# Second group's keys, grams and inversion ahead of the first FFN block of a delta rule with two FFN layers

## The chip, the cores and the metric

One core of one Trainium2 chip runs the whole program. Five engines work side by side, each through its own queue in order: TensorE (PE, matrix products; PEld is its weight load), VectorE (DVE), ScalarE (ACT), GpSimd (POOL) and SyncE (SP, which here only issues DMAs). An engine waits for another by semaphores. The metric is the time of one execution on the device in microseconds; lower is better.

## What is computed

```python
k_n = k / (norm(k) + 1e-6)                    # (4, 8, 768, 48): batch, head, time, dim
for t in range(768):                          # the delta rule, one state (48 x 48) per batch and head
    y[t]  = q[t] @ state
    v_old = state.T @ k_n[t]
    state = state + beta[t] * outer(k_n[t], v[t] - v_old)
x = y as (3072 tokens, 384)
h = x @ w_in                                  # (384, 2048)
g = 0 below -1, (h + 1)**2 / 4 between, h above 1
x = g @ w_out                                 # (2048, 384)
h = x @ w_in2;  g = relu(h)**2;  out = g @ w_out2
```

The time loop is done in 24 chunks of 32 steps. Within a chunk the steps depend on each other through a triangular matrix per batch and head, which is inverted; between chunks they depend through the state.

## The kernel before

**Chunks and groups.** A chunk holds 32 time steps of all 32 batch-head pairs. Chunks are gathered in groups of 2, 4, 4, 4, 4, 4, 2 (`GROUPS`). For each chunk `gram(c)` makes the products of keys with keys and of queries with keys on PE (L302, 64 matmuls), ACT or DVE takes them out of PSUM, and a mask is multiplied in (L318, on POOL where `eng=G`). For each group `tri(n, eng)` inverts all its triangles at once: `begin` transposes the grams to `gm` (L394, DVE), `pre` makes norms and scales two matrices (L266 to L434), `steps` is a chain of `tensor_mul` to `t` and `tensor_add` to `tx` (L454, L455), and `end` transposes back (L458). Groups 0 and 1 are done in halves (28 instructions instead of 60), with two small products for the rest: `rows` transposes `d` (L483), `ld` makes `z` (L487), `dld` makes `w` (L495) and subtracts it (L500). Group 0 is inverted on DVE, all later groups on POOL.

**A chunk's chain.** `chunk_steps(c)` gives six steps, called ks, tr, qs, ku, pu, xt below: what the state already predicts is subtracted from the value (L532), the inverse is applied (L536, copied by ACT L544), the output is made (L522, L556, copied by L560), the state moves on (L567, copied by L572 and L573), and `xt` turns the output into the FFN's input, a high part `xh` and a low part `xl` in fp32r (L590 to L593). Its tr needs the inverse of the chunk's group; `value(c)` (L278, POOL) multiplies the norms into the values.

**FFN units.** The FFN runs in blocks of chunks (`SIZES` 2, 2, 3, ...) and, in a block, in 16 units, one for each 128 columns of the hidden width. `unit(x)` does `hidden` (nine matmuls to `h`, then r on ACT L631, g on DVE L632, ACT L634, DVE L635), `rest` (high part `gh` on ACT L644, low part `gl` on DVE L646) and, two units later, `out1` (nine matmuls to `acc`). From unit 4 until the first layer's last block `h` has one PSUM bank, so the next unit's `h` waits for this unit's r. Units 0 to 15 are the first block and use chunks 0 and 1; units 16 to 31 use chunks 2 and 3.

**Weights on the way.** The weights of the first layer come as 64-bit integers and are made into fp32r pairs during the first block: two ACT instructions for each of 32 tiles (`whole_bits`, L170 and L173), `make` on DVE (L180), `upper` (L214, a cast on ACT or POOL) and `lower` (L219, DVE). `between(f)` hangs two tiles, a and b, on each unit. `EARLY` tiles have their bits done before unit 0, tiles below `READY` are complete before it.

**The order.** It is written by hand: `put_a(0, slot, ...)` hangs work ahead of `rest` (even slot) or behind `out` (odd slot) of a unit, `put` behind `rest` or at the unit's end; slot s belongs to unit s // 2. Everything up to unit 15 is issued in that order on every engine; from unit 16 on only PE's order is fixed. The slots that the change touches are `begin1`, `pre1`, `steps1` (the second group's inversion, POOL), `rows1`, `ld1`, `dld1`, the steps of chunks 2 and 3, and the grams of group 2 (chunks 6 to 9), from whose last slot (`ready`) `tri_put` places the third group's inversion: `begin` one slot later, `steps` five slots later, `end` in slot 48, ahead of chunk 6.

Of the kernel before, what the change touches and what calls it, by code (L numbers as in the profile page):

```python
# [21 lines left out]
GROUPS = [2, 4, 4, 4, 4, 4, 2]  # L22
# [3 lines left out]
def kernel(  # L26
# [350 lines left out]
    def tri(n, eng, halves=False):  # L377
        x = tx
        gm = ring.tile([P, T, T], F32, tag="gm", bufs=1, name="gm")
# [36 lines left out]
        def row():  # L416
            if halves:
                d = two(gm, both, both)
                eng.tensor_mul(
                    d, d, r.rearrange("p (a o i) -> p a o i", a=2, o=1)  # L420
                    .to_broadcast([P, 2, T2, T2]))
                return
            for e, rs, cs in whole:
                e.tensor_mul(gm[:, rs, cs], gm[:, rs, cs], across(r, rs, cs))

        def row2():
            if halves:
                eng.tensor_mul(
                    two(x, both, both), two(gm, both, both),
                    g.rearrange("p (a i o) -> p a i o", a=2, o=1).to_broadcast([P, 2, T2, T2]))  # L430
# [283 lines left out]
    EARLY, READY, HELD = 9, 3, 6  # L714
# [11 lines left out]
    def between(f):  # L726
        a, b = tiles[2 * f:2 * f + 2]

        def part(x):
            if x == 0:  # L730
                if last_low:
                    lower(last_low.pop(), V)
                if a is not None:
                    make(a)
                some(2)
            elif x == 1:
                if a is not None:
                    upper(a, nc.scalar.copy)
                if b is not None:
                    make(b)  # L740
            elif x == 2:
                if b is not None:
                    upper(b, G.tensor_copy)
                    last_low.append(b)
                some(2)
            elif a is not None:
                lower(a, V)

        return part
# [45 lines left out]
    with tc.manual_schedule():  # L795
        for c in range(HEADS):
# [3 lines left out]
        among = {  # L800
            1: lambda: load_kq(2), 2: lambda: load_kv(1), 3: lambda: load_kq(3),
            4: lambda: load_kg(KQ), 6: lambda: load_kg(KQ + 1), 8: lambda: load_kv(HEADS),
        }
        for x in range(NW - HELD):
            among.get(x, lambda: None)()
            load_w(order[x])
        G.memset(zero, 0.0)
# [24 lines left out]
        whole_bits(0)
        cross_gram(0, 1)
        whole_bits(1)
        masks.append(gram(3, late=2, eng=G))
        for x in range(2, 5):
            whole_bits(x)
# [3 lines left out]
        after(value(0), ins)  # L841
        value(1)
        for c in range(HEADS):
            mask_of_head(c)
        go(masks)
        chains = [chunk_steps(c) for c in range(HEADS)]
        (s0, t0, q0, p0, k0, x0), (s1, t1_, q1, p1, k1, x1) = chains
        ld0(0)
        ld0(1)
        make(0)  # L850
        make(1)
        dld0(0)
        dld0(1)
        upper(0, nc.scalar.copy)
        upper(1, nc.scalar.copy)
        make(2)
        whole_bits(5)
        s0()
        t0()
        lower(0, V)  # L860
        lower(1, V)
        upper(2, nc.scalar.copy)
        whole_bits(6)
        s1()
        t1_()
        lower(2, V)
# [3 lines left out]
        whole_bits(7)  # L870
# [3 lines left out]
        whole_bits(8)  # L874
        turn[0] = None

        chunk2, chunk3 = [], []
        begin1, pre1, steps1, end1 = tri(1, G, True)
        masks1 = []
        put(0, 0, lambda: (save1(0), save1(1)))  # L880
        put_a(0, 0, lambda: masks1.append(gram(4, late=2, eng=G)))
        put(0, 1, lambda: go(masks1[:1]))
        put_a(0, 2, lambda: masks1.append(gram(5, late=2, eng=G)))
        put(0, 2, lambda: go(masks1[1:]))
        put_a(0, 3, k0)
        put(0, 4, lambda: (save1(2), save1(3)))
        put_a(0, 5, k1)
        put(0, 5, begin1, lambda: go(pre1[:4]), lambda: go(pre1[4:7]), lambda: go(pre1[7:]))
        put(0, 4, lambda: [load_kg(KQ + KG + c) for c in range(KG)])
# [12 lines left out]
        for c, at_ in ((2, (12, 20, 21, 22, 23, 25)), (3, (24, 26, 27, 28, 29, 30))):  # L902
# [121 lines left out]
```

## Time and profile before

| | us |
|---|---|
| median of 3 runs | 1064.01 (1063.97 to 1064.74) |
| profiled execution, own time | 1062.24 |
| its span | 1060.5 |
| PE busy | 1000.5 (94%) |
| DVE, ACT, POOL busy | 580.6, 474.4, 294.0 |
| first `h` of unit 0 starts | 45.56 |
| chunk 6's tr on PE | 183.89 |

PE is the busiest engine, and in 40 slices of the span it is at nine tenths or more in all but about the first nine. So the time is PE's work plus what PE waits or runs slowly in the first 184 us. A row of a timeline gives start, length, engine, line, operation, and in brackets the idle time ahead of it and who ended it; a row of the windows gives busy time by engine, the granted clock of TensorE (1.00 is 2.4 GHz, 0.50 is 1.2 GHz) and the DMA traffic.

### The profile page before, as it was taken

How to read it: one execution, taken by the hardware profiler on the slowest of the kernel's cores; microseconds unless marked ns; L12 is line 12 of the kernel's file. 1: busy time of each engine (PE TensorE's matmuls, PEld its weight loads, DVE VectorE, ACT ScalarE, POOL GpSimd, SP SyncE). 2: the span in 40 equal slices, each digit the busy share in tenths (PEclk: the TensorE clock that was granted, in tenths of full speed). 3: DMA queues.
4: the chain of work that ended last, by engine and by line, in shares of the span. 5: the costliest groups of instructions: out<-in, count | busy, mean ns of one | idle time of the engine just before them, and what ended most of it. 6: DMA issues, size and time to landing. Idle time of an engine off the chain costs nothing.

```text
span 1060.5 us, 33708 instructions
## 1 busy us (share of the span) xinstructions
PE 1000.5 (94%) x14824; PEld 955.0 (90%) x14824; DVE 580.6 (55%) x1064; ACT 474.4 (45%) x989; POOL 294.0 (28%) x440
## 2 busy tenths in 40 slices
PE   5776887999999999999999999999999999999998
PEld 4665777899899998999999999999999999999998
DVE  6386666575575656657645577643434343434333
ACT  3474445454454544545445554433333333333332
POOL 3144087086029407707700123110101010110000
PEclk9985899999999999999999999999999999999999
DMA  9681245343351451522012223010101010000000
GB/s 255 211 230 46 63 129 154 97 136 91 103 156 54 136 147 45 158 63 69 17 35 75 76 90 119 16 45 1 45 1 46 1 45 1 23 1 23 1 23 23
DMA packets 36051, 80.93 MB, mean 76 GB/s; under 512 B 4544, under 2 KB 18368, under 8 KB 35904
## 3 DMA queue, kind: packets, MB, share of 16 engines
q1 hardware_dynamic: 35904, 78.78, 25.0%
q8 instruction: 116, 1.90, 0.7%
q14 instruction: 31, 0.25, 0.1%
HBM read 63.03 MB, written 15.73 MB: 74 GB/s over the span
## 4 chain that ended last, share of the span: by engine, by line
PE 82%; DVE 4%; POOL 3%; issue 1%; ACT 1%; DVEq 0%; ACTq 0%; POOLq 0%
PE acc L605 36%; PE h L605 35%; PE g L302 2%; PE sps L567 1%; PE tr L536 1%; PE yy L522 1%; PE yy L556 1%; POOL tx L455 1%; POOL t L454 1%; PE ks L522 1%; DVE gl L646 1%; PE xt L590 1%; DVE g L632 1%; DVE gm L394 0%; DVE g L635 0%
## 5 line engine op out<-in xcount | busy, mean ns | idle before, releaser
L605 PE MATMUL h<-xh,w 128*128 128x384 f32 (+1 forms) x1632 | 321.7, 333 | 11.0 <-ACT r L631 8.6
L605 PEld LDWEIGHTS h<-xh,w 128*128 128x128 f32 x1632 | 273.2, 190 | 16.8 <-ACT r L631 9.7
L646 DVE TENSOR_TENSOR gl<-g,gh 128x384 fp32r<-128x384 f32 (+1 forms) x272 | 172.2, 633 | 140.2 <-ACT gh L644 131.9
L644 ACT CAST gh<-g 128x384 fp32r<-128x384 f32 (+1 forms) x272 | 134.5, 494 | 208.2 <-DVE g L635 90.2
L605 PE MATMUL h<-xl,w 128*128 128x384 f32 (+1 forms) x816 | 179.5, 329 | 1.3 <-DVE xl L593 1.3
L605 PE MATMUL acc<-gh,w 128*128 128x384 f32 (+1 forms) x864 | 169.9, 333 | 0.6 <-issue 0.6
L605 PE MATMUL acc<-w,gh 128*128 128x384 f32 x768 | 156.4, 339 | 1.9 <-DVE e L654 1.9
L639 DVE TENSOR_TENSOR g<-r 128x384 f32<-128x384 f32 x128 | 71.3, 557 | 157.9 <-ACT r L638 157.9
L638 ACT ACTIVATE r<-h,zero 128x384 f32<-128x384 f32 x128 | 74.3, 580 | 167.2 <-PE h L605 167.2
L605 PEld LDWEIGHTS acc<-gh,w 128*128 128x128 f32 x864 | 138.6, 193 | 6.0 <-issue 1.4
L605 PEld LDWEIGHTS h<-xl,w 128*128 128x128 f32 x816 | 141.2, 190 | 1.9 <-DVE xl L593 1.9
L605 PEld LDWEIGHTS acc<-w,gh 128*128 128x128 f32 x768 | 137.0, 188 | 2.2 <-ACT gh L644 2.2
L631 ACT ACTIVATE r<-h,one 128x384 f32<-128x384 f32 (+1 forms) x144 | 78.3, 544 | 88.5 <-PE h L605 88.1
L635 DVE SCALAR_TENSOR_TENSOR g<-r,g 128x384 f32<-128x384 f32 (+1 forms) x144 | 88.8, 617 | 40.5 <-ACT g L634 39.0
L632 DVE TENSOR_SCALAR g<-r 128x384 f32<-128x384 f32 (+1 forms) x144 | 61.1, 424 | 82.2 <-ACT r L631 81.3
L455 POOL TENSOR_TENSOR tx<-tx,t 128x58 f32<-128x58 f32 (+9 forms) x164 | 97.6, 595 | 12.5
L634 ACT ACTIVATE g<-g 128x384 f32<-128x384 f32 (+1 forms) x144 | 70.2, 488 | 62.7 <-DVE g L632 62.0
L454 POOL TENSOR_TENSOR t<-tx,gm 128x58 f32<-128x58 f32 (+9 forms) x164 | 93.3, 569 | 16.1 <-DVE tx L433 4.0
L605 PE MATMUL acc<-gl,w 128*128 128x384 f32 (+1 forms) x432 | 91.8, 322 | 0.0
L696 POOL CAST xh<-x2r 128x1152 fp32r<-128x1152 f32 x8 | 9.4, 1171 | 293.0 <-PE h L605 246.1
L605 PE MATMUL acc<-w,gl 128*128 128x384 f32 x384 | 88.4, 338 | 0.0
L605 PEld LDWEIGHTS acc<-gl,w 128*128 128x128 f32 x432 | 73.3, 193 | 0.0
(103 smaller groups left out, 850.0 us busy)
## 6 DMA issues: line engine op xcount, KB each, us to landing
raw<-in_w_dram SPq DMA_DIRECT2D x64, 384.0 KB, 3.9
kqt<-in_kq_dram SPq DMA_DIRECT2D x88, 192.0 KB, 3.8
kv<-in_kv_dram SPq DMA_DIRECT2D x24, 384.0 KB, 3.0
w2f<-wl SPq DMA_DIRECT2D x32, 192.0 KB, 3.7
w2r<-w2f SPq DMA_DIRECT2D x16, 384.0 KB, 3.0
x2r<-x SPq DMA_DIRECT2D x8, 576.0 KB, 4.3
out_dram<-e SPq DMA_DIRECT2D x24, 192.0 KB, 2.0
x<-e SPq DMA_DIRECT2D x18, 192.0 KB, 2.9
```

The source lines that it names most:

```text
L302: nc.tensor.matmul(g[p, h].rearrange("p x i -> p (x i)"), x[:, 0:T], x[:, lo * T:hi * T], start=h == 0, stop=True, skip_group_check=True,)
L454: eng.tensor_mul(t, by.to_broadcast(shape), of.to_broadcast(shape))
L455: return eng.tensor_add(rest, rest, t)
L605: nc.tensor.matmul(o, *((r, l) if swap else (l, r)), **flags)
L631: marks[0] = nc.scalar.activation(r, h, AF.Relu, bias=one)
L632: marks[1] = nc.vector.tensor_scalar(g, r, 2.0, 0.5, ALU.min, ALU.mult)
L634: nc.scalar.activation(g, g, AF.Square)
L635: nc.vector.scalar_tensor_tensor(g, r, -1.0, g, ALU.add, ALU.max)
L638: marks[0] = nc.scalar.activation(r, h, AF.Relu, bias=zero)
L639: marks[1] = nc.vector.tensor_mul(g, r, r)
L644: nc.scalar.copy(ghi, g)
L646: nc.vector.tensor_sub(glo, g, ghi.bitcast(F32))
```

## The change

The second group's keys are loaded ahead of the weights, its grams (chunks 4, 5; those of 2 and 3 were there) are made beside the first group's inversion, and its four masks run on POOL in one row. `begin1`, `pre1` and all of `steps1` stand in the first chunks' chain, ahead of unit 0; the two scalings in `pre1` go from POOL to DVE (`first=V`). 12 weight tiles instead of 9 have their bits done, and 5 instead of 3 are complete, before unit 0; in units 0 to 3 the second tile's `upper` goes from POOL to ACT, and `lower` of the tile before stands behind `make`. Within the first block, `rows1`, `ld1`, `dld1` and the steps of chunks 2 and 3 stand at earlier slots, one at each; the grams of group 2 stand at slots 10, 18, 22, 24 instead of 13, 16, 19, 22.

```diff
-    def tri(n, eng, halves=False):
+    def tri(n, eng, halves=False, first=None):
         x = tx
+        first = first or eng
...
         def row():
             if halves:
-                eng.tensor_mul(
+                first.tensor_mul(
...
-    EARLY, READY, HELD = 9, 3, 6
+    EARLY, READY, HELD = 12, 5, 6
...
             if x == 0:
-                if last_low:
-                    lower(last_low.pop(), V)
                 if a is not None:
                     make(a)
                 some(2)
...
                 if b is not None:
                     make(b)
+                if last_low:
+                    lower(last_low.pop(), V)
             elif x == 2:
                 if b is not None:
-                    upper(b, G.tensor_copy)
+                    upper(b, G.tensor_copy if f > 3 else nc.scalar.copy)
...
-        among = {
-            1: lambda: load_kq(2), 2: lambda: load_kv(1), 3: lambda: load_kq(3),
-            4: lambda: load_kg(KQ), 6: lambda: load_kg(KQ + 1), 8: lambda: load_kv(HEADS),
-        }
+        for c in range(HEADS, KQ):
+            load_kq(c)
+        for c in range(KG):
+            load_kg(KQ + c)
+        among = {1: lambda: load_kv(1), 8: lambda: load_kv(HEADS)}
         for x in range(NW - HELD):
             among.get(x, lambda: None)()
             load_w(order[x])
+            if x in (14, 16):
+                load_kg(KQ + KG + (x - 14) // 2)
...
+        masks += [gram(c, late=2, eng=G) for c in range(KQ, KQ + KG)]
+        for x in range(3):
             whole_bits(x)
         ins = go(steps)
         rows0()
         end()
         after(value(0), ins)
+        go(masks)
         value(1)
         for c in range(HEADS):
             mask_of_head(c)
-        go(masks)
...
+        begin1, pre1, steps1, end1 = tri(1, G, True, V)
...
+        for c in range(GROUPS[1]):
+            save1(c)
+        begin1()
         s0()
         t0()
-        lower(0, V)
-        lower(1, V)
-        upper(2, nc.scalar.copy)
-        whole_bits(6)
+        lower(2, V)
+        pre1[0]()
+        whole_bits(7)
+        whole_bits(8)
         s1()
         t1_()
-        lower(2, V)
+        go(pre1[1:])
+        steps1[0]()
+        value(2)
+        go(steps1[1:])
+        lower(3, V)
+        make(4)
+        upper(4, nc.scalar.copy)
+        whole_bits(9)
+        whole_bits(10)
+        lower(4, V)
         q1()
...
-        put_a(0, 3, k0)
-        put_a(0, 5, k1)
-        put(0, 5, begin1, lambda: go(pre1[:4]), lambda: go(pre1[4:7]), lambda: go(pre1[7:]))
-        put(0, 7, lambda: [load_w(order[x]) for x in range(NW - HELD, NW)])
+        put_a(0, 1, k0)
+        put_a(0, 3, k1)
+        put(0, 5, lambda: [load_w(order[x]) for x in range(NW - HELD, NW)])
+        put(0, 6, rows1, end1)
...
-        for i, f in enumerate(steps1):
-            put(0, 8 + i // 2, f)
-        put(0, 10, lambda: value(2))
-        put(0, 15, rows1, end1)
-        put(0, 17, lambda: value(3))
-        put_a(0, 16, lambda: ld1(0), lambda: ld1(1))
-        put_a(0, 17, lambda: ld1(2), lambda: ld1(3))
-        put_a(0, 18, lambda: dld1(0), lambda: dld1(1))
-        put_a(0, 22, lambda: dld1(2), lambda: dld1(3))
-        for c, at_ in ((2, (12, 20, 21, 22, 23, 25)), (3, (24, 26, 27, 28, 29, 30))):
+        put(0, 11, lambda: value(3))
+        put_a(0, 7, lambda: ld1(0), lambda: ld1(1))
+        put_a(0, 8, lambda: ld1(2), lambda: ld1(3))
+        put_a(0, 9, lambda: dld1(0), lambda: dld1(1))
+        put_a(0, 25, lambda: dld1(2), lambda: dld1(3))
+        for c, at_ in ((2, (5, 11, 12, 13, 14, 16)), (3, (15, 17, 19, 20, 21, 23))):
...
-            ready[c] = 13 + 3 * i
+        for c, slot in zip(range(GFIRST[2], GFIRST[3]), (10, 18, 22, 24)):
+            ready[c] = slot
```

How that moves instructions is shown at three places. Line numbers of the changed kernel are one higher in `tri`, `joined`, `chunk_steps` and `hidden`.

POOL, from the masks of the grams (L318, `gp<-gp,mask`) to the first steps of the second group's inversion (`t<-tx,gm`), before; `w<-wl` is the cast of a weight tile in a unit:

```order
L318 TENSOR_TENSOR gp<-gp,mask 128x8x2x32 x2
L214 CAST w_886<-wl 128x384
L318 TENSOR_TENSOR gp<-gp,mask 128x8x2x32
L214 CAST w_957<-wl 128x384
L318 TENSOR_TENSOR gp<-gp,mask 128x8x2x32
L214 CAST w_1026<-wl 128x384
L214 CAST w_1117<-wl 128x384
L214 CAST w_1181<-wl 128x384
L419 TENSOR_TENSOR gm<-gm,st_824 128x2x16x16
L428 TENSOR_TENSOR tx<-gm,st_823 128x2x16x16
L454 TENSOR_TENSOR t<-tx,gm 128x28
```

The same place in the changed kernel (`kv<-kv,nt` is `value`, the 128x256 masks are those of the first two chunks):

```order
L278 TENSOR_TENSOR kv<-kv,nt 128x384
L318 TENSOR_TENSOR gp<-gp,mask 128x8x2x32 x4
L278 TENSOR_TENSOR kv<-kv,nt 128x384
L352 TENSOR_TENSOR gp<-gp,mask 128x256 x2
L455 TENSOR_TENSOR t<-tx,gm 128x28
L456 TENSOR_TENSOR tx<-tx,t 128x2x14
```

The casts of units 0 to 4 and the two scalings are gone from between the masks and the steps, and no unit's work stands ahead of the steps any more.

DVE, where the second group's inverse comes back from POOL (`d<-tx`), between unit 7 and unit 8 before:

```order
L646 TENSOR_TENSOR gl<-g,gh 128x256
L219 TENSOR_TENSOR w_1422<-wl,w_1422 128x384
L483 STREAM_TRANSPOSE d<-tx 128x16x32
L632 TENSOR_SCALAR g<-r 128x256
L219 TENSOR_TENSOR w_1429<-wl,w_1429 128x384
```

and between unit 3 and unit 4 in the changed kernel:

```order
L647 TENSOR_TENSOR gl<-g,gh 128x256
L219 TENSOR_TENSOR w_1227<-wl,w_1227 128x384
L484 STREAM_TRANSPOSE d<-tx 128x16x32
L459 STREAM_TRANSPOSE gp<-tx 128x32x32
L633 TENSOR_SCALAR g<-r 128x256
```

The transposition moved four units up, and the second one (`gp<-tx`), which stood behind unit 8, now follows it at once, ahead of unit 4's g.

DVE, where the third group's inversion begins (`gm<-gp`), before; the `g<-r` behind it is unit 12's:

```order
L318 TENSOR_TENSOR gp<-g,mask 128x8x2x32
L646 TENSOR_TENSOR gl<-g,gh 128x256
L219 TENSOR_TENSOR w_1951<-wl,w_1951 128x384
L394 STREAM_TRANSPOSE gm<-gp 128x32x32
L632 TENSOR_SCALAR g<-r 128x256
```

and in the changed kernel, where the `g<-r` behind it is unit 13's:

```order
L318 TENSOR_TENSOR gp<-g,mask 128x8x2x32
L647 TENSOR_TENSOR gl<-g,gh 128x256
L219 TENSOR_TENSOR w_2255<-wl,w_2255 128x384
L501 TENSOR_TENSOR gp<-gp,w 128x8x16 x2
L395 STREAM_TRANSPOSE gm<-gp 128x32x32
L633 TENSOR_SCALAR g<-r 128x256
```

It moved one unit down. PE's order from unit 15 on, and DVE's, ACT's and POOL's from about unit 25 on, read alike in both kernels.

## Rows read from the trace of the kernel before

**Rows 1.** Busy time by engine in five stretches, then TensorE's clock and DMA.

```profile
0.00:45.56 45.56, 25.22 (x967) 21.78 (x967) 21.39 (x55) 16.76 (x38) 11.24 (x29) 1.00 0.81 237
45.56:91.55 45.99, 29.62 (x519) 26.66 (x520) 35.75 (x72) 31.86 (x77) 22.74 (x41) 0.84 0.63 182
91.55:144.66 53.11, 44.93 (x1421) 40.98 (x1422) 35.14 (x74) 22.24 (x55) 12.45 (x23) 0.76 0.19 51
144.66:183.89 39.23, 33.14 (x882) 30.14 (x881) 24.64 (x44) 19.71 (x50) 32.58 (x52) 1.00 0.57 166
183.89:1060.50 876.61, 867.55 (x11037) 835.43 (x11037) 463.64 (x822) 383.80 (x772) 214.94 (x296) 1.00 0.20 60
```

**Rows 2.** PE's timeline: four rows with the wait ahead of each.

```profile
23.84 1.90 PE L487 MATMUL z<-d,l 32*32 32x16 f32 x128 [4.37 <-DVE d L483]
...
45.56 1.65 PE L605 MATMUL h<-xh,w 128*128 128x256 f32 x6 [0.57 <-ACT xh L592]
...
91.55 1.90 PE L487 MATMUL z<-d,l 32*32 32x16 f32 x128 [5.91 <-DVE g L632]
...
183.89 0.88 PE L536 MATMUL tr<-kv,gp 32*32 32x48 f32 x64 [2.97 <-DVE kv L532]
```

**Rows 3.** POOL, 72.5 to 90.4 us by line: busy, mean ns, idle.

```profile
L455 POOL TENSOR_TENSOR tx<-tx,t 128x28 f32<-128x28 f32 (+6 forms) x14 | 6.2, 444 | 1.1
```

**Rows 4.** Timeline, DVE row behind those steps.

```profile
90.36 1.04 DVE L483 STREAM_TRANSPOSE d<-tx 128x512 f32<-128x512 f32 x1 [2.31 <-POOL tx L455]
```

**Rows 5.** Timeline, third group's inversion: begin on DVE, POOL's first and last step.

```profile
124.53 2.15 DVE L394 STREAM_TRANSPOSE gm<-gp 128x1024 f32<-128x1024 f32 x1
...
139.02 0.23 POOL L454 TENSOR_TENSOR t<-tx,gm 128x30 f32<-128x30 f32 x1
...
179.74 0.28 POOL L455 TENSOR_TENSOR tx<-tx,t 128x30 f32<-128x30 f32 x1
```

**Rows 6.** Timeline of the first chunks' chain: preparation on DVE, subtraction, copy on ACT.

```profile
11.54 0.35 DVE L267 RECIPROCAL st<-st 128x32 f32<-128x32 f32 x1 [0.42 <-ACT st L266]
...
14.88 0.18 DVE L454 TENSOR_TENSOR t<-tx,gm 128x28 f32<-128x28 f32 x1
...
36.54 0.55 DVE L532 TENSOR_TENSOR kv<-kv,ks 128x384 f32<-128x384 f32 x1 [3.24 <-issue]
...
43.56 0.47 ACT L560 COPY kv<-yy 128x384 f32<-128x384 f32 x1
```

**Rows 7.** Timeline, a mask on POOL and two DVE rows, beside and behind it.

```profile
51.06 1.45 POOL L318 TENSOR_TENSOR gp<-gp,mask 128x512 f32<-128x512 f32 x1
...
51.31 1.62 DVE L219 TENSOR_TENSOR w<-wl,w 128x384 fp32r<-128x384 f32 x1
...
53.06 0.55 DVE L219 TENSOR_TENSOR w<-wl,w 128x384 fp32r<-128x384 f32 x1
```

**Rows 8.** ACT's timeline, r of units 0, 6, 7, 10, 11 and 12.

```profile
47.89 0.47 ACT L631 ACTIVATE r<-h,one 128x256 f32<-128x256 f32 x1 [1.50 <-PE h L605]
...
76.95 0.46 ACT L631 ACTIVATE r<-h,one 128x256 f32<-128x256 f32 x1
...
81.63 0.45 ACT L631 ACTIVATE r<-h,one 128x256 f32<-128x256 f32 x1
...
109.47 0.47 ACT L631 ACTIVATE r<-h,one 128x256 f32<-128x256 f32 x1 [1.97 <-PE h L605]
...
113.58 0.47 ACT L631 ACTIVATE r<-h,one 128x256 f32<-128x256 f32 x1 [0.23 <-PE h L605]
...
126.19 0.47 ACT L631 ACTIVATE r<-h,one 128x256 f32<-128x256 f32 x1 [0.74 <-PE h L605]
```

**Rows 9.** A stretch by windows, columns as in Rows 1.

```profile
83.50:107.40 23.90, 17.18 (x511) 15.72 (x515) 14.00 (x28) 10.04 (x25) 7.84 (x18) 0.50 0.07 20
```

**Rows 10.** PE's timeline, `h` of units 9 and 10, six of nine matmuls.

```profile
100.45 1.65 PE L605 MATMUL h<-xh,w 128*128 128x256 f32 x6
...
108.05 0.97 PE L605 MATMUL h<-xh,w 128*128 128x256 f32 x6
```

More of the change, by code (lines that the diff above doesn't have):

```diff
@@ L427, in row2 @@
             if halves:
-                eng.tensor_mul(
+                first.tensor_mul(
                     two(x, both, both), two(gm, both, both),
@@ L829 @@
         go(pre[1:])
+        cross_gram(0, 1)
+        masks.append(gram(3, late=2, eng=G))
         for c in range(HEADS):
             save0(c)
[L832 to L836, printed above, removed]
+        masks += [gram(c, late=2, eng=G) for c in range(KQ, KQ + KG)]
+        for x in range(3):
             whole_bits(x)
@@ L844 @@
             mask_of_head(c)
-        go(masks)
         chains = [chunk_steps(c) for c in range(HEADS)]
         (s0, t0, q0, p0, k0, x0), (s1, t1_, q1, p1, k1, x1) = chains
+        begin1, pre1, steps1, end1 = tri(1, G, True, V)
         ld0(0)
         ld0(1)
-        make(0)
-        make(1)
+        for x in range(3):
+            make(x)
+        whole_bits(3)
+        upper(0, nc.scalar.copy)
+        lower(0, V)
+        make(3)
+        upper(1, nc.scalar.copy)
+        whole_bits(4)
+        lower(1, V)
+        upper(2, nc.scalar.copy)
+        whole_bits(5)
+        upper(3, nc.scalar.copy)
         dld0(0)
         dld0(1)
[L854 to L857, printed above, removed]
-        s0()
-        t0()
-        lower(0, V)
-        lower(1, V)
-        upper(2, nc.scalar.copy)
-        whole_bits(6)
+        whole_bits(6)
+        for c in range(GROUPS[1]):
+            save1(c)
+        begin1()
+        s0()
+        t0()
+        lower(2, V)
+        pre1[0]()
+        whole_bits(7)
+        whole_bits(8)
         s1()
         t1_()
-        lower(2, V)
+        go(pre1[1:])
[8 more added lines that the diff above has]
+        lower(4, V)
         q1()
@@ L869 @@
         p0()
-        whole_bits(7)
         p1()
@@ L873 @@
         x1()
-        whole_bits(8)
+        whole_bits(11)
         turn[0] = None
[L877 to L884, printed above, removed]
-        put_a(0, 3, k0)
-        put(0, 4, lambda: (save1(2), save1(3)))
-        put_a(0, 5, k1)
-        put(0, 5, begin1, lambda: go(pre1[:4]), lambda: go(pre1[4:7]), lambda: go(pre1[7:]))
-        put(0, 4, lambda: [load_kg(KQ + KG + c) for c in range(KG)])
-        put(0, 7, lambda: [load_w(order[x]) for x in range(NW - HELD, NW)])
+        put_a(0, 1, k0)
+        put_a(0, 3, k1)
+        put(0, 5, lambda: [load_w(order[x]) for x in range(NW - HELD, NW)])
+        put(0, 6, rows1, end1)
         for c in range(HEADS):
             put(0, 8 + c, lambda c=c: load_kq(c + KQ))
-        for i, f in enumerate(steps1):
-            put(0, 8 + i // 2, f)
-        put(0, 10, lambda: value(2))
-        put(0, 15, rows1, end1)
-        put(0, 17, lambda: value(3))
-        put_a(0, 16, lambda: ld1(0), lambda: ld1(1))
-        put_a(0, 17, lambda: ld1(2), lambda: ld1(3))
-        put_a(0, 18, lambda: dld1(0), lambda: dld1(1))
-        put_a(0, 22, lambda: dld1(2), lambda: dld1(3))
-        for c, at_ in ((2, (12, 20, 21, 22, 23, 25)), (3, (24, 26, 27, 28, 29, 30))):
+        put(0, 11, lambda: value(3))
[4 more added lines that the diff above has]
+        for c, at_ in ((2, (5, 11, 12, 13, 14, 16)), (3, (15, 17, 19, 20, 21, 23))):
             def steps_of(c=c, box={}):
@@ L911 @@
         at, ready = {}, {}
-        for i, c in enumerate(range(GFIRST[2], GFIRST[3])):
-            ready[c] = 13 + 3 * i
+        for c, slot in zip(range(GFIRST[2], GFIRST[3]), (10, 18, 22, 24)):
+            ready[c] = slot
             put_a(0, ready[c], lambda c=c: gram(c))
```

## The prediction

> **What bounds the kernel now.** I read the stretches first [rows 1]. From 183.89 us to the end PE is busy 867.6 of 876.6 us at full clock; the change touches nothing there, and PE's order is the same. What can be won lies before: from the first `h` at 45.56 [rows 2] to 183.89 PE is busy 107.7 of 138.3 us, and in two of the three stretches the clock stands at 0.84 and 0.76 of full. Then PE's waits [rows 2]: 5.9 us ahead of `z` at 91.55 and 3.0 us ahead of chunk 6's tr at 183.89. The releaser printed at 91.55 is g; what came last is `d` on DVE, which itself waited 2.3 us for POOL's last step [rows 4]. So unit 8 was held by the second group's inversion, and the clock was at 0.50 from 83.5 to 107.4 [rows 9]; six matmuls of `h` take 1.65 us there and 0.97 after [rows 10]. Then the third group: it begins on DVE at 124.53, POOL steps from 139.02 to 180.02 [rows 5], and 3.9 us later PE gets its tr. Between these, units are paced by ACT and DVE with the weights: 4.7 us from r to r with POOL stepping beside them (76.95 to 81.63), 4.1 without (109.47 to 113.58) [rows 8]. PE's share of a unit, two times nine matmuls, is below that at full clock.
>
> **The change part by part.** I carry one execution's clock forward to chunk 6's tr, since all behind it is unchanged.
>
> *Ahead of unit 0.* The two added grams are 128 matmuls in the wait of 4.4 us ahead of 23.84 [rows 2]; they cost nothing as long as they are done before group 0's `z`, and about what that row's 128 matmuls take, 1.9 us, if not. POOL does value 0, four masks of 1.45 us [rows 7], value 1: chunk 1's subtraction, which needs value 1, is at 36.54 [rows 6], some 6 us later than POOL is through, so that is free. SP: eight half loads of keys (1.5 MB) go ahead of the first weight; at 237 GB/s [rows 1] that is 6.5 us for the first weights, and keys 2 to 5 were loaded between the first weights anyway, so from the seventh tile on only the two further key loads (3.2 us) remain. The first bits move behind the grams; ACT needs three tiles before 25 us. I take zero, upper bound 3. The six held weights are issued two units earlier, their spare tiles are free after ku of chunk 1, which also moved up; zero.
>
> Behind the subtraction at 36.54, DVE now prepares the second group: norms to scaled matrices took 3.3 us for group 0 (11.54 to 14.88) [rows 6], so about 40.6 us. Then `lower`, `make` (0.55 each with no POOL beside, [rows 7]), and on ACT a cast and four bit instructions, five of about 0.47 like the copy in [rows 6], 2.3 us, ahead of the two output copies, the last of which was at 43.56 [rows 6] and would now be near 44.6. **First `h`: 46.5, 1 us later**; bounds 0 and 4, the upper if masks and steps hold DVE (below).
>
> *A rule that speaks against it.* A DVE subtraction beside a mask took 1.62 us instead of 0.55 [rows 7]: it waited for the mask to end. The Trainium skill, SBUF — State Buffer, "Who interferes with whom", says that a DVE instruction with two SBUF inputs and a GpSimd instruction that reads SBUF take an exclusive lock for their whole length. By that rule the ten `make` and `lower` ahead of unit 0 could each wait out a mask or step, while by the row only one DVE instruction waits per mask and small steps hold little; by the rule alone it is the last rival below.
>
> *Units 0 to 3.* POOL's 28 steps are 12.4 us busy and about 2 idle (14 additions 6.2 and 1.1 [rows 3], the products as much), plus value 2: from 40.7 to about 57. So units 0, 1, 2 run with POOL beside: 4.7 us each. r of unit 0 is 2.3 us behind `h` (45.56 to 47.89 [rows 2, 8]): 48.8; r of unit 3: 63. Casts of units 0 to 3 move to ACT, 0.5 us each, but grams' copies, `save1` and the norms leave these units; I set them against each other.
>
> *The second group comes back.* `rows1` stands behind unit 3's last DVE row: 63 + 4.1 + 1.0 (`d`, [rows 4]) = 68.1. POOL is done ten us before, so POOL no longer decides. But PE has `z` ahead of unit 4's `h`, and has nothing else: it idles some 6 us again, and the clock will be at 0.50 as at 91.55. `z` 1.9 [rows 2] and `h` 2.5 (1.65 for six of nine, [rows 10]): r of unit 4 at 72.6. Then `z`, `acc`, `w`, `h` at half clock, 1.9 + 2.5 + 1.9 + 2.5: r of unit 5 at 81.4 (before: 87.56 was unit 8's; so this place costs the same as before, only earlier).
>
> *Units 5 to 12.* One or two chunk steps in each, evenly; PE stays under 4.4 us a unit at full clock. 4.1 and 0.2 for the odd gram mask: 7 x 4.3 = 30.1; **r of unit 12 at 111.5 instead of 126.19** [rows 8], 14.7 us earlier. Bounds: 4.1 everywhere and full clock sooner, 105; 4.9, 117.
>
> *The third group.* Its `begin` now stands behind unit 12's DVE work, not ahead of it, and its steps two slots later. Before, steps came 12.8 us after r of unit 12 (139.02 - 126.19). Add one unit, 4.1; take off four weight instructions of 0.55 that left units 13 and 14: 14.7. Steps start at 126.2. They are the same 60 instructions beside the same DVE work: 44.9 us to chunk 6's tr (183.89 - 139.02 [rows 2, 5]). One more value stands inside the steps, and `end` stands a little better in DVE's row; I let them cancel (each under 2 us). **tr at 171.1 instead of 183.9: 12.8 us.** PE will be there sooner than before relative to POOL: units 12 to 15 lost nearly all their chunk steps. It then waits 9 us or more, where it waited 3.0, and this time the clock should fall: 2.5 us lost, bounds 0 and 4.
>
> Sum: 12.8 - 2.5 = **10.3 us**. Against the execution's own 1062.24 that is 1051.9; the median lies 1.8 higher (1064.01), so **1053.7**.
>
> **The rivals.**
> *PE decides, not POOL.* If the third group's steps start as soon as before after r of unit 12 (12.8) and units keep 4.1, tr comes at 105 + 12.8 + 44.9 = 162.7, 21 us earlier, with a shorter wait and no clock loss: 1043. For it: POOL is empty from 57 us on but for casts. Against it: `begin` moved down a unit in DVE's row, and steps wait for its scalings.
> *The gain is taken back at the third group.* If steps begin as late as before, because unit 12 comes only 4 us earlier or values hoisted between the steps wait for their loads (value 7 needs chunk 4's last step, and POOL gets there some 2 us after it by my count), tr stays within 2 us of 183.9: 1063.
> *Slower: POOL holds the first chunks' chain.* Four masks (5.8 us) and 28 steps now stand beside DVE's `make` and `lower` at 25 to 46 us, which precede the subtractions of that serial chain in DVE's row. At 1.07 us each (1.62 - 0.55 [rows 7]), twelve of them delay the first `h` by 13 us, and the weights' order behind it, so units 0 to 2 too, by 1 us each. From a first `h` at about 58 on nothing is left of the 12.8; at 59, with the clock's 2.5 us: 1068. For it: one row of each kind was slowed so. Against it: DVE stood idle 3.2 us ahead of 36.54 while PE waited for nothing that the profile shows [rows 6], so it has slack there.
>
> **How the numbers follow.** Forecast 0.69, PE decides 0.10, taken back 0.09, slower 0.12. The forecast's own range, from the bounds of first `h` (0 to 4), unit 12 (105 to 117), steps after unit 12 (12.8, or that and a whole unit, 16.9) and clock (0 to 4), not all at one end, is a gain of 3 to 20 us, 1044 to 1061. For 8 in 10 I take 1043 to 1062. A measurement here tells 0.2% (2.1 us) from no change. Faster than 1061.9: most of the forecast and the first rival, 0.77; same 0.10; slower 0.13.
>
> **What would show it.** First `h` at 46 to 47; `d` behind unit 3 with no wait for POOL; no PE wait near unit 8; r of unit 12 near 111; POOL's third-group steps from about 126 to 167; PE's wait ahead of chunk 6's tr grown from 3 to about 9 us, followed by a stretch at 0.50. If that wait is gone, the first rival holds; if the first `h` is past 55, the last. Wrong would be above all that units 0 to 12 keep about 5 us, or that POOL's 41 us of steps change length.

## The result, and the profile after

The changed kernel takes **1052.28 us** (median of four runs, 1050.14 to 1056.35) against 1064.38 for the kernel before (1063.97 to 1065.07): a ratio of 0.989, 95% interval 0.986 to 0.9921, so faster by about 12 us, well outside the 0.2% that can be told from no change. Run again later in other company it took 1052.63 against 1064.03, ratio 0.9894 (0.9874 to 0.9915). The forecast was 1053.7. The profiled execution took 1050.14 us, its span is 1048.4.

The stretches, cut where [rows 1] were cut: first `h`, then the second group's return, the end of the half clock behind it, r of unit 12, chunk 6's tr. Columns as there (busy time of PE, PEld, DVE, ACT and POOL, clock, DMA share, GB/s).

```profile
0.00:47.23 47.23, 27.58 (x1094) 24.44 (x1094) 31.40 (x71) 22.91 (x53) 19.99 (x44) 0.98 0.82 225
47.23:66.98 19.75, 13.46 (x246) 12.42 (x247) 14.61 (x32) 16.44 (x39) 7.50 (x17) 0.76 0.80 239
66.98:82.50 15.52, 15.10 (x478) 14.00 (x479) 6.62 (x14) 6.39 (x17) 0.71 (x1) 0.50 0.78 221
82.50:110.06 27.56, 27.26 (x847) 24.78 (x850) 24.04 (x53) 21.53 (x51) 6.76 (x9) 1.00 0.35 93
110.06:169.61 59.55, 44.95 (x1137) 41.34 (x1130) 40.07 (x81) 26.49 (x65) 40.95 (x67) 0.93 0.44 128
169.61:1048.40 878.79, 869.55 (x11037) 837.58 (x11037) 461.86 (x819) 383.77 (x770) 215.69 (x296) 1.00 0.20 59
```

tr came at 169.61 instead of 183.89, 14.3 us earlier, and the rest behind it takes 878.79 instead of 876.61, 2.2 us more: together the 12.1 us between the two executions. PE's waits that answer to [rows 2], from its timeline (start, length, work, and the wait ahead of it in brackets):

```profile
33.27 1.50 PE L537 MATMUL tr<-kv,gp 32*32 32x48 f32 x64 [3.11 <-DVE gp L501]
...
47.23 1.65 PE L606 MATMUL h<-xh,w 128*128 128x256 f32 x6 [0.57 <-ACT xh L593]
...
66.98 1.90 PE L488 MATMUL z<-d,l 32*32 32x16 f32 x128 [5.50 <-DVE d L484]
...
169.61 1.50 PE L537 MATMUL tr<-kv,gp 32*32 32x48 f32 x64 [8.83 <-issue]
```

The wait ahead of z has only moved, from 91.55 to 66.98; the one ahead of tr has grown from 2.97 to 8.83. DVE's `d` waits for nothing now (against 2.31 for POOL in [rows 4]), and the third group's inversion, [rows 5], lies 13 us earlier on POOL:

```profile
65.81 1.03 DVE L484 STREAM_TRANSPOSE d<-tx 128x512 f32<-128x512 f32 x1
...
115.21 2.20 DVE L395 STREAM_TRANSPOSE gm<-gp 128x1024 f32<-128x1024 f32 x1
...
125.82 0.23 POOL L455 TENSOR_TENSOR t<-tx,gm 128x30 f32<-128x30 f32 x1
...
167.20 0.26 POOL L456 TENSOR_TENSOR tx<-tx,t 128x30 f32<-128x30 f32 x1
...
167.50 2.01 DVE L459 STREAM_TRANSPOSE gp<-tx 128x1024 f32<-128x1024 f32 x1 [4.75 <-POOL tx L456]
```

PE's row names no releaser for its wait ahead of tr; these rows show it: POOL's last step, then `gp<-tx` on DVE, idle 4.75 us for it and done at 169.51, then tr at 169.61.

The rows of r that answer to [rows 8], units 0, 3, 4, 5 and 12:

```profile
49.56 0.47 ACT L632 ACTIVATE r<-h,one 128x256 f32<-128x256 f32 x1 [1.48 <-PE h L606]
...
62.06 0.45 ACT L632 ACTIVATE r<-h,one 128x256 f32<-128x256 f32 x1
...
71.20 0.47 ACT L632 ACTIVATE r<-h,one 128x256 f32<-128x256 f32 x1 [1.99 <-PE h L606]
...
80.21 0.47 ACT L632 ACTIVATE r<-h,one 128x256 f32<-128x256 f32 x1 [3.67 <-PE h L606]
...
110.06 0.47 ACT L632 ACTIVATE r<-h,one 128x256 f32<-128x256 f32 x1 [0.60 <-PE h L606]
```

### The profile page after: what moved, and what is told of

Same layout as the page of the kernel before. It is cut to its first block, busy times and chain, and to the rows that moved or that the text cites. A ratio compares the mean times of both kernels' runs of the same rounds, so it can differ in the third digit from the quotient of the medians.

```text
span 1048.4 us, 33710 instructions
## 1 busy us (share of the span) xinstructions
PE 997.9 (95%) x14824; PEld 954.6 (91%) x14824; DVE 578.6 (55%) x1066; ACT 477.5 (46%) x994; POOL 291.6 (28%) x433
## 4 chain that ended last, share of the span: by engine, by line
PE 83%; DVE 6%; DMA 6%; issue 2%; ACT 2%; SPq 0%; POOL 0%; DVEq 0%; ACTq 0%; POOLq 0%
PE acc L606 36%; PE h L606 36%; DMA raw<-in_w_dram 5%; PE g L302 2%; PE tr L537 2%; PE yy L557 2%; PE sps L568 2%; PE yy L523 2%; PE ks L523 1%; DVE gl L647 1%; DVE g L636 1%; ACT gh L645 1%; DVE g L633 1%; PE xt L591 1%; DMA kqt<-in_kq_dram 1%
## 5 line engine op out<-in xcount | busy, mean ns | idle before, releaser
L606 PEld LDWEIGHTS acc<-gl,w 128*128 128x128 f32 x432 | 72.5, 190 | 0.0
```

What stands on the lines that cost most here:

```text
L606: nc.tensor.matmul(o, *((r, l) if swap else (l, r)), **flags)
```

## Experiments

The theory at the start: all of the gain is the second group's inversion leaving the units; what is left lies in two waits, PE ahead of z (5.50 us, with half clock behind it) and PE ahead of chunk 6's tr (8.83 us, set by POOL). The rivals: PE's own work ahead of `begin` bounds by now; other parts of the change (weights, casts, spread steps) carry it; POOL holds the first chunks' chain. Every edit is to the changed kernel. `tr` stands for the start of chunk 6's tr, and ratios are to the kernel before in the same company, with 95% intervals.

**What carries the gain: the steps put back into the units.**

```
-        steps1[0]()
-        value(2)
-        go(steps1[1:])
...
-        put(0, 6, rows1, end1)
+        for i, f in enumerate(steps1):
+            put(0, 8 + i // 2, f)
+        put(0, 10, lambda: value(2))
+        put(0, 15, rows1, end1)
```

(with ld1 at 16 and 17, dld1 at 18 and 22, value 3 at 17, and the chunks' slots as before the change)

> Edit: the second group's steps on POOL go back into units 4 to 10, its return behind unit 7 and the steps of chunks 2 and 3 to their old slots; preparation, grams, masks, keys and weights stay as changed. Theory (the steps' place carries all of the gain): r of unit 12 at 118 to 127 instead of 110.06, the third group's steps from 132 to 140, tr at 177 to 184; 1059 to 1066 us. Rival (earlier weights, loads and preparation carry a part of it by themselves): tr at 171 to 176; 1053 to 1058 us.

Measured: 1061.6 us against 1064.03, ratio 0.9977 (0.9964 to 0.999). The third group's steps start at 136.45, and PE's two waits are back in the old places:

```profile
87.04 1.90 PE L488 MATMUL z<-d,l 32*32 32x16 f32 x128 [8.10 <-DVE g L633]
...
180.31 1.50 PE L537 MATMUL tr<-kv,gp 32*32 32x48 f32 x64 [4.49 <-DVE kv L533]
```

So of the 11.4 us that the changed kernel gained in the same company (1064.03 to 1052.63), 9.0 hang on the place of those steps, together with what this edit moves along with them: the return, z and w, and the chunks' slots. Earlier weights, loads, grams and preparation by themselves are worth 2.4 us (1.1 to 3.8 by the interval). The loss is not in the units beside the steps: r of unit 8 comes at 81.88 here, 12.2 us sooner than in the changed kernel (94.12), where the return lies ahead of it. It lies behind the return: r of unit 8 to r of unit 12, with z, w and the bunched chunk steps in it, takes 38.5 us (to 120.34), against 15.9.

**The even spread of chunks 2 and 3 undone.**

```
-        for c, at_ in ((2, (5, 11, 12, 13, 14, 16)), (3, (15, 17, 19, 20, 21, 23))):
+        for c, at_ in ((2, (12, 20, 21, 22, 23, 25)), (3, (24, 26, 27, 28, 29, 30))):
```

> Edit: the steps of chunks 2 and 3 stand at the slots of the kernel before (12 to 25 and 24 to 30); all else as changed. Theory (what lies behind POOL's start is free until tr, what lies ahead of it is not): six steps leave the units ahead of begin, about 4 to 6 us of PE work; steps start at 120 to 122 instead of 125.82, tr at 164 to 166, PE's wait there 1 to 5 us; 1045 to 1049 us. Rival (the even spread is a gain by itself, since bunched steps lengthen their units on PE and DVE): begin as late as now, tr at 169 to 173; 1050 to 1056 us.

Measured: 1052.01 us, ratio 0.9886 (0.9864 to 0.9908): no difference. Units 5 to 11 do get shorter (3.3 us each from r of unit 6 to r of unit 11, the first two rows), r of unit 12 comes at 107.10, but units 13 and 14 with the bunched steps are longer:

```profile
84.59 0.48 ACT L632 ACTIVATE r<-h,one 128x256 f32<-128x256 f32 x1 [0.37 <-PE h L606]
...
101.12 0.48 ACT L632 ACTIVATE r<-h,one 128x256 f32<-128x256 f32 x1
...
107.10 0.48 ACT L632 ACTIVATE r<-h,one 128x256 f32<-128x256 f32 x1 [0.78 <-PE h L606]
115.92 0.47 ACT L632 ACTIVATE r<-h,one 128x256 f32<-128x256 f32 x1 [1.59 <-PE h L606]
120.64 0.47 ACT L632 ACTIVATE r<-h,one 128x256 f32<-128x256 f32 x1 [1.29 <-PE h L606]
```

POOL's first step is at 125.95, tr at 169.77. What the theory left out: POOL's first step hangs on scalings that stand in DVE's row behind units 13 and 14, so work moved from ahead of `begin` into these units delays POOL just the same. The even spread does nothing for the time that these runs can tell.

**The third group's grams earlier.**

```
-        for c, slot in zip(range(GFIRST[2], GFIRST[3]), (10, 18, 22, 24)):
+        for c, slot in zip(range(GFIRST[2], GFIRST[3]), (10, 13, 16, 19)):
```

> Edit: the third group's grams stand at slots 10, 13, 16 and 19 instead of 10, 18, 22 and 24; begin then stands behind unit 10's row on DVE and POOL's steps some two and a half units earlier. Theory (POOL's inversion of the third group sets chunk 6's tr, which came at 169.61 us with PE waiting 8.83 us): steps start about 10 us earlier (115 to 118 us instead of 125.82), tr at 160 to 163, PE's wait there 0 to 2 us, no stretch at half clock; 1040 to 1045 us. Rival (PE's own work is the bound by now, the wait is only where its slack shows): tr moves by less than 3 us and the wait reappears at another place before it; 1049 to 1053 us.

Measured: 1050.6 us, ratio 0.9871 (0.984 to 0.9903), not to be told from the changed kernel. The theory's numbers fail: r of unit 10 comes at 110.11, where r of unit 12 had been (110.06), so what `begin` gained in units the units lost in length; POOL's first step is at 126.75, and tr is late:

```profile
173.01 0.91 PE L537 MATMUL tr<-kv,gp 32*32 32x48 f32 x64 [2.68 <-DVE kv L533]
```

The rival's direction holds, though tr moved by 3.4 us, not by less than 3. It is PE that has no room ahead of `begin`: from r of unit 4 to r of unit 10 (70.98 to 110.11) it is busy 34.33 of 39.13 us, and 3.7 of the rest are waits without a releaser; DVE and ACT are busy 22.12 and 22.84. This profile is the slowest of its four executions (1052.77), so how much the earlier grams cost is not shown.

**The casts of units 0 to 3 back on POOL.**

```
-                    upper(b, G.tensor_copy if f > 3 else nc.scalar.copy)
+                    upper(b, G.tensor_copy)
```

> Edit: the second cast of units 0 to 3 goes to POOL as in the kernel before, behind the second group's steps, instead of to ACT. Theory (ACT is busy without a break from 55.9 to 66 us and paces units 2 and 3; the casts could stand on POOL once its steps are done at 55.98): units 0 and 1 up to 1.5 us later, units 2 and 3 half a us shorter each, r of unit 4 between 70 and 72.5, tr within 2 us of 169.61; 1050 to 1054 us. Rival (the cast behind POOL's steps holds DVE's lower and with it g and h of unit 2): r of unit 3 at 65 or later instead of 62.06, tr 3 to 6 us later; 1054 to 1058 us.

Measured: 1052.93 us, ratio 0.9906 (0.988 to 0.9931). r of units 0 to 3 at 49.64, 53.03, 56.77 and 62.75: unit 3 a little late, not the 3 us of the rival. tr is at 175.28, outside what either had, in the slowest of the four executions (1054.26), with 3.9 us of waits without a releaser between r of units 4 and 6. In the median this part of the change neither gains nor costs that these runs can tell.

**POOL's masks done twice.**

```
         go(masks)
+        go(masks)
```

> Edit: the four gram masks on POOL are done twice (values 0 and 1, so the same result), 5.6 us more of POOL beside the first chunks' chain. Theory (DVE has slack there, POOL's work beside it costs little): first h later by 0 to 1.5 us, the second group's steps start where they did (41.15) or up to 2 us later, tr within 2 us of 169.61; 1050 to 1054 us. Rival (POOL holds the chain at 1.07 us an instruction): first h at 51.5 us, 4.3 us later, and the same again at r of units 0 to 3; 1056 to 1060 us.

Measured: 1053.05 us, ratio 0.9902 (0.9875 to 0.9928); first r 1.4 us later (50.93), tr at 172.53, 0.9 past the theory's bound. DVE's timeline, first of the changed kernel, then with the masks twice; the first row of each is a `lower` beside a mask or value, which takes 0.5 us alone, the second is what PE's tr waits for:

```profile
29.74 1.18 DVE L219 TENSOR_TENSOR w<-wl,w 128x384 fp32r<-128x384 f32 x1
...
32.84 0.47 DVE L501 TENSOR_TENSOR gp<-gp,w 128x128 f32<-128x128 f32 x2
```

```profile
29.60 1.62 DVE L219 TENSOR_TENSOR w<-wl,w 128x384 fp32r<-128x384 f32 x1
...
34.22 0.47 DVE L501 TENSOR_TENSOR gp<-gp,w 128x128 f32<-128x128 f32 x2
```

The hold that [rows 7] showed is there: three instructions that had taken 1.07 to 1.18 us take 1.61 to 1.62, 1.5 us in sum. That is, to 0.1 us, L501's delay (34.22 for 32.84) and the first r's. The rest of the added POOL time lies beside work or waits of DVE that it doesn't lengthen: 1.4 us, not 4.3.

**z behind unit 4's h, and the second group's return two units earlier.** Two tries at taking PE's 5.50 us wait away:

```
-        put_a(0, 7, lambda: ld1(0), lambda: ld1(1))
-        put_a(0, 8, lambda: ld1(2), lambda: ld1(3))
-        put_a(0, 9, lambda: dld1(0), lambda: dld1(1))
+        put_a(0, 8, lambda: ld1(0), lambda: ld1(1))
+        put_a(0, 9, lambda: ld1(2), lambda: ld1(3))
+        put_a(0, 10, lambda: dld1(0), lambda: dld1(1))
```

> Edit: the second group's z and w products stand one slot later, behind unit 4's h instead of ahead of it. Theory (PE waits 5.50 us at 66.98 us because z was put ahead of an h that was ready): r of unit 4 comes at about 66.5 instead of 71.20 us, the wait ahead of z shrinks under 1.5 us, the stretch at half clock from 65.5 to 82.5 shortens, unit 12's r and with it begin, POOL's steps and tr come 4 to 8 us earlier; 1044 to 1048 us. Rival (ACT and the weights' loads pace units 3 to 5, not z): r of unit 5 stays within 2 us of 80.21, tr within 2 us of 169.61; 1051 to 1053 us.

```
-        put(0, 6, rows1, end1)
+        put(0, 4, rows1, end1)
```

(and ld1 at 5 and 6, dld1 of the first two chunks at 7)

> Edit: the second group's return from POOL (rows1, end1 on DVE, then z and w on PE) stands two units earlier, behind unit 2's row, with z ahead of and behind unit 3's h; POOL's steps are done at 55.98 us, before that. Theory (PE's 5.50 us wait at 66.98 comes only from the place of d in DVE's row): d at about 62 instead of 65.81, PE's wait ahead of z under 2 us, r of unit 5 at 73 to 76 instead of 80.21, r of unit 12 at 102 to 106 instead of 110.06, steps from 118 to 122, tr at 162 to 166; 1044 to 1049 us. Rival (that time is lost to the 256 small products of z and w and the half clock beside them, wherever they stand, as the run with z behind h4 suggests, where r of unit 4 came 5.5 us earlier and r of unit 6 3.7 us later): r of unit 12 within 2 us of 110.06, tr within 2 us of 169.61; 1050 to 1053 us.

Measured: 1054.07 us (0.9905, 0.9879 to 0.993) and 1052.64 (0.9902, 0.9879 to 0.9925). Neither gains. z in the first run, then in the second:

```profile
66.60 1.65 PE L488 MATMUL z<-d,l 32*32 32x16 f32 x128 [1.89 <-DVE d L484]
```

```profile
64.28 1.90 PE L488 MATMUL z<-d,l 32*32 32x16 f32 x128 [5.65 <-DVE d L484]
```

In the first, r of unit 4 comes at 65.65 as the theory had it, yet r of unit 6 at 89.59. The clock stands at 0.50 until 91.0 there (82.54 in the changed kernel), DVE's `gp` makes PE wait 1.57 us ahead of a gram, and waits without a releaser sum up to 2.80 us from z to r of unit 6 (0.41). In the second the wait was not taken away: `d` came at 63.11 for the 62 expected. r of unit 6 is at 85.19; then 3.37 us of wait without a releaser follow, and r of unit 12 is at 115.65, in the slowest of its six executions. From z to r of unit 6 it is 23.0 and 20.9 us, against 18.9 in the changed kernel and 21.0 in the repeat below. An earlier z did not bring a gain; which of these causes took it is not separated.

**PE kept busy in its two waits.**

```
             o = att([P, H, T2], "z")
+            if n == 1 and c == 0:
+                warm(o, 70, 0)
...
             o = att([P, H, D], "tr")
+            if c == 6:
+                warm(o, 55, 1)
```

(`warm(o, n, i)` issues n matmuls of `xh` into the tile that the next products overwrite)

> Edit: PE gets idle work (matmuls whose result is overwritten) in its two long waits: 70 of 128 columns ahead of the first z (5.50 us of wait at 66.98) and 55 of 256 columns ahead of chunk 6's tr (8.83 us at 169.61). Theory (those waits are what lets the clock fall to half, from 65.47 to 82.54 and from 164.46 to 174.70): no stretch at half clock there; r of unit 6 at 79 to 82 instead of 85.86, and from tr to the end 876.5 instead of 878.8 us; 1045 to 1049 us. Rival (the clock falls with the small products of z and w themselves, whatever stands ahead, or the kept time is lost elsewhere): half clock for over 12 us between 65 and 92 all the same, r of unit 6 at 85 to 90; 1050 to 1054 us.

Measured: 1053.57 us, ratio 0.9908 (0.9884 to 0.9932). Ahead of tr the idle work was done at once and 6.25 us of wait were left; from tr on it took 878.49. Ahead of z it kept the clock, which stands at 1.00 from 47 to 66.98 and at 0.74 to 82.50, instead of 0.76 and 0.50. But r of unit 6 is at 87.80. The timeline of PE, with DVE's `d` between:

```profile
60.90 7.93 PE L514 MATMUL z<-xh,w 128*128 128x128 f32 x70
...
65.31 1.06 DVE L484 STREAM_TRANSPOSE d<-tx 128x512 f32<-128x512 f32 x1
...
68.76 1.28 PE L490 MATMUL z<-d,l 32*32 32x16 f32 x128
...
71.23 0.84 PE L490 MATMUL z<-d,l 32*32 32x16 f32 x79
74.83 0.84 PE L490 MATMUL z<-d,l 32*32 32x16 f32 x49 [2.76 <-issue]
```

The first z takes 1.28 us at full clock instead of 1.90, and from z to r of unit 4 it is 2.64 us instead of 4.22 (71.20 less 66.98). But the idle work ran to 68.8, while `d` was done at 66.37: it held z back by about 2.3 us and so took its own gain back, r of unit 4 coming at 71.40. Behind it lie a wait of 2.76 us that has no releaser (the repeat below has 2.96 in this stretch without any idle work) and, from 74.38, the half clock again. So this run shows no gain, but it does not show that the half clock costs nothing here.

**The changed kernel again**, to see how far one program's executions differ.

> Edit: none, the changed kernel again, since the run with the last steps on DVE, alike up to unit 12, reached r of unit 6 at 89.55 us where the changed kernel's profile had 85.86. Theory (waits for nothing that the profile shows, and the length of the half-clock stretch, differ from execution to execution of one program by some 4 us): r of unit 6 anywhere from 84 to 91, single times spread over 4 us or more; from r of unit 6 to r of unit 12 24 to 25.2 us and from there to tr 59.0 to 60.0 as before. Rival (executions agree within a microsecond and that edit reached back ahead of unit 12): r of unit 6 within 1 us of 85.86.

Measured: single times from 1051.05 to 1053.48, a spread of 2.4 us, less than the theory's 4; first r 49.55 and r of unit 4 71.24, within 0.04 of the first profile, then r of unit 6 at 88.04 (85.86), tr at 171.79 (169.61). From r of unit 6 to r of unit 12 it is 24.4 us (24.2 in the first profile), from there to tr 59.4 (59.6). The 2.2 us arise here; first the changed kernel's profile, then the repeat:

```profile
71.03 0.50 PE L488 MATMUL z<-d,l 32*32 32x16 f32 x21
71.95 1.67 PE L488 MATMUL z<-d,l 32*32 32x16 f32 x107 [0.41 <-issue]
...
75.78 2.12 PE L496 MATMUL w<-gp,z 32*32 32x16 f32 x128
...
83.44 1.06 PE L537 MATMUL tr<-kv,gp 32*32 32x48 f32 x64
```

```profile
71.07 0.51 PE L488 MATMUL z<-d,l 32*32 32x16 f32 x21
72.50 1.68 PE L488 MATMUL z<-d,l 32*32 32x16 f32 x107 [0.92 <-issue]
...
76.32 0.39 PE L496 MATMUL w<-gp,z 32*32 32x16 f32 x11
77.19 1.78 PE L496 MATMUL w<-gp,z 32*32 32x16 f32 x117 [0.48 <-issue]
...
84.02 0.82 PE L537 MATMUL tr<-kv,gp 32*32 32x48 f32 x57
86.40 0.28 PE L537 MATMUL tr<-kv,gp 32*32 32x48 f32 x7 [1.56 <-issue]
```

0.41 us of waits without a releaser in one, 2.96 in the other: enough for the whole difference. And they fall at the same places of the program, 128 matmuls apart (107, nine of `acc` and 11 make 127, one record missing; from there to the third, 117, 9, 64, 9 and 57, are 256). Ahead of unit 0 it is the same: over the eleven executions here whose program is alike up to there, its r lies anywhere from 48.05 to 50.78. A single profile thus tells 2 us in one of these stretches from nothing only where rows show the cause.

**The last steps of the third group on DVE.**

```
-            eng.tensor_mul(t, by.to_broadcast(shape), of.to_broadcast(shape))
-            return eng.tensor_add(rest, rest, t)
+            e = nc.vector if n == 2 and j >= 20 else eng
+            e.tensor_mul(t, by.to_broadcast(shape), of.to_broadcast(shape))
+            return e.tensor_add(rest, rest, t)
```

> Edit: the last 11 of the third group's 30 steps (22 instructions, from 154.11 to 167.46 us on POOL) run on DVE, which is idle for 4.75 us ahead of 167.50. Theory (the inversion's length on POOL sets chunk 6's tr): 22 instructions of about 0.3 us instead of 0.6, tr at 163 to 166 instead of 169.61, PE's wait there 3 to 6 instead of 8.83 us, half clock behind it shorter; 1045 to 1049 us. Rival (the steps on DVE hold back g and gl of the units beside them, so PE reaches tr later): tr at 168 to 171, wait under 6 us with waits ahead of h or acc of blocks before it grown as much; 1050 to 1054 us.

Measured: 1050.3 us, ratio 0.9889 (0.9863 to 0.9915), the changed kernel's own ratio, so the times show no gain; the profile does. Up to unit 12 the program is the same, so the stretch behind its r is compared: 57.25 us to tr instead of 59.4 to 59.6, and 4.99 us of wait instead of 7.5 to 8.8. DVE's row shows why it is 2.2 and not 6:

```profile
167.40 1.05 DVE L648 TENSOR_TENSOR gl<-g,gh 128x256 fp32r<-128x256 f32 x1
168.38 0.20 DVE L457 TENSOR_TENSOR tx<-tx,t 128x58 f32<-128x58 f32 x1
168.62 0.20 DVE L456 TENSOR_TENSOR t<-tx,gm 128x30 f32<-128x30 f32 x1
```

A step takes 0.2 to 0.4 us there instead of 0.3 to 0.8, but stands in DVE's order behind a unit's `gl`. The theory's direction holds: POOL's inversion does set tr.

**Both together.** The edits of the second group's return two units earlier and of the last steps on DVE.

> Edit: both the second group's return two units earlier and the third group's last 11 steps on DVE. Theory (two waits, one behind the other on PE's path): the gains add, tr at 156 to 161 instead of 169.61; 1037 to 1044 us. Rival (PE or ACT is the bound once either wait is gone): no more than the better of the two alone, 1045 to 1050 us.

Measured: 1048.73 us, ratio 0.9871 (0.985 to 0.9892); r of unit 6 at 85.86 and of unit 12 at 110.26, as in the changed kernel, tr at 167.36. So the 2.2 us of the steps on DVE are there again, and the earlier return adds nothing that the trace shows; the interval still overlaps the changed kernel's.

**Fewer small products between d and `begin`.** In that kernel, z and w of chunks 4 and 5, which the next block uses first:

```
-        put_a(0, 6, lambda: ld1(2), lambda: ld1(3))
-        put_a(0, 25, lambda: dld1(2), lambda: dld1(3))
+        put_a(0, 26, lambda: ld1(2), lambda: ld1(3))
+        put_a(0, 28, lambda: dld1(2), lambda: dld1(3))
```

> Edit: the kernel with the second group's return two units earlier and the third group's last steps on DVE, and in it z and w of the group's last two chunks (of which chunk 4 is the first user, in the next block) move from units 3 and 12 to units 13 and 14, where PE waits for POOL anyway. Against that kernel's profile (r of unit 4 78.62, unit 6 85.86, unit 12 110.26, tr 167.36). Theory (from d to r of unit 6 PE is bound by the number of small products, which it gets no faster than 128 in some 4 us): r of unit 6 at 81 to 84, r of unit 12 at 106 to 108.5, tr at 163 to 165.5; 1043 to 1047 us. Rival (ACT and the weights pace these units, or the products only change places with another wait): r of unit 12 within 1.5 us of 110.26, or tr within 1.5 us of 167.36; 1047 to 1050 us.

Measured: **1046.67 us**, ratio 0.983 (0.9806 to 0.9854), below both intervals of the changed kernel and the best of all; from the kernel that it was made of (0.985 to 0.9892) the intervals do not separate it. The profiled execution is the slowest of its six (1048.77): r of unit 6 is at 83.33, inside the theory's range, then r of unit 12 at 112.91 and tr at 169.12, outside it. PE's timeline:

```profile
79.13 0.82 PE L538 MATMUL tr<-kv,gp 32*32 32x48 f32 x57
81.69 0.28 PE L538 MATMUL tr<-kv,gp 32*32 32x48 f32 x7 [1.73 <-issue]
...
85.23 0.66 PE L569 MATMUL sps<-kv 32*48 32x48 f32 x39
89.53 0.49 PE L569 MATMUL sps<-kv 32*48 32x48 f32 x25 [3.64 <-issue]
```

Again 128 matmuls apart (7, 9, 64, 9, 39). The median carries the verdict, and it agrees with the theory's time; that the saved products are its cause is not shown. r of unit 6 comes 2.5 us earlier than in the kernel that it was made of, but 1.1 of these lay ahead of unit 0 already (first r 48.48 for 49.54), and behind unit 6 the profile is later than that kernel's.

## Why the prediction was right

**Ahead of unit 0.** First `h` at 47.23 for 46.5. One thing was not in the sum. Three `make` took 4.04 us together and two `lower` with a fourth `make` 1.07 to 1.18 each beside masks and values, so PE, through with w at 30.15, got its tr only at 33.27, behind L501, and chunk 1's subtraction came at 37.39 for 36.54; the slack had been thought to take all of that. Then xt waited 1.70 us for ACT, which had a cast and four bit instructions ahead of the output copies; that was foreseen, as 1 us. The last rival's mechanism was real, but `h` came 1.7 us later than before, not 13. The rule of the Trainium skill that was weighed there (SBUF — State Buffer, "Who interferes with whom") agrees with these rows. Beside the small steps `make` and `lower` took 0.51 to 0.76 us, against 0.55 in [rows 7].

**Units 0 to 3.** r of unit 3 at 62.06 for 63, z at 66.98 for 68.1. `d` had no POOL wait, as forecast. The price of a unit with POOL beside was too high: 4.2 us (49.56 to 62.06 for three), not 4.7. The late first `h` hid part of that.

**The second group's return.** r of unit 4 at 71.20 for 72.6, of unit 5 at 80.21 for 81.4. The terms hold too: z, `h`, z, `acc`, w and `h` have their half-clock lengths in PE's timeline (1.90 for z, 1.65 for six matmuls of `h` or `acc`). What the sum had no term for are the waits without a releaser, 0.41 us here and 2.96 in the repeat. Whether PE's wait and the half clock could be won back is open: of the three tries, one left the wait in place, one kept the half clock longer, and one held z back itself.

**Units 5 to 12.** 29.9 us for 30.1, r of unit 12 at 110.06 for 111.5. This number is right by luck, for the mechanism was wrong. The forecast had DVE and ACT with the weights pace a unit at 4.1, and PE below that. But PE is busy 27.26 of the 27.56 us from 82.50 to 110.06 (DVE 24.04, ACT 21.53), and with the chunk steps moved out of these units, the weights unchanged, a unit took 3.3 us. So PE's own work set the pace, and chunk steps in these units do cost time. Nor does it help that the steps lie evenly: bunched, the kernel is as fast.

**The third group.** Steps from 125.82 for 126.2, POOL through at 167.46 for 167, tr at 169.61 for 171.1 (171.79 in the repeat), wait 8.83 for 9. Steps began 15.8 us after r of unit 12, for 14.7; from the first step to tr it took 43.8, for 44.9. Three values stood between the steps, one more than before, 2.8 us in all, and `end` followed POOL closer; they cancelled, as assumed. The clock behind tr was at half to 174.70 and the rest took 2.2 us more than before, for 2.5; in the repeat 0.9 more (877.51).

**The sum.** 10.3 us foreseen, 12.1 measured (11.4 in the repeat). The total is closer than its terms: the late first `h`, the shorter units 0 to 3, the later start of POOL's steps and the earlier tr behind them are each off by 0.7 to 1.7 us, and largely cancel. The first rival, PE deciding, is out as a whole, since the steps did not begin 12.8 us after r of unit 12 and PE's wait ahead of tr grew; as a bound ahead of `begin` it holds, by PE's busy time there. The second, the gain taken back at the third group, is out.

## What to carry to other kernels

Move a serial chain of a slow engine to where the other engines wait anyway, and look for the gain where that engine's next chain is awaited, here chunk 6's tr, 14.3 us earlier; the wait of the moved chain's own consumer may only move along (5.91 us before, 5.50 after). About four fifths of the gain came from moving 28 small POOL instructions with the return and the products that wait for them, and none that the runs can tell from the careful spread of the rest. Then ask which stretch of an engine's order the next start hangs on: work shifted within that stretch changed nothing here; work taken out of it gave the best time, though not by more than the intervals allow. And check which engine paces a stretch by taking its work out, since a pace that fits can have another cause. Run one kernel twice before reading two profiles against each other.

## What the runs showed of the hardware

PE waits that name no releaser (`issue`), those ahead of chunk 6's tr aside, lie mostly in stretches of small products, at places 128 matmuls or a multiple of that apart, 0.3 to 3.7 us each, and differ between executions of one program. With a weight load to each matmul that is every 256 instructions; the page of the changed kernel lists the larger of two queues of instruction loads (packets, MB, share) as

```profile
q8 instruction: 116, 1.90, 0.8%
```

so 16.4 KB a packet, and 116 times 256 is PE's 29,648 matmuls and weight loads within a fifth of a per cent. The traces show when these packets came: in the fourteen profiled executions, each of the 128 such waits of 0.3 us or more in the first 190 us ends 1.1 to 1.8 us after a packet of this queue ended (in the changed kernel the packet at 70.53, the wait at 71.95). So what PE waits for there is its next instructions. The Trainium skill, Runtime: NRT & Kernel Launch, "Instruction fetch mechanics", says that instructions come in blocks of 256, that the next is fetched while the current one runs, and that the cost of crossing into it is mostly hidden. The block agrees with the places; that it is hidden does not hold in these stretches, where such waits sum up to 8 us between 62 and 90 us of one execution. Why a load comes late in one execution and not in another stays open: no run here changed what else is on the DMA engines at that time.

A kept clock can end in the same waits: with PE busy up to 68.76 us the clock fell at 74.38 instead of 65.47, inside the 2.76 us for which PE then waited without a releaser, as it had fallen inside the 5.50 us ahead of z in the changed kernel.
